# Attention decode with a gated mix: V products and output projection spread over column groups of TensorE, one V buffer instead of a rotation, products taken in their own iteration

## Chip, cores, metric

One core of a Trainium2 chip. The metric is the device time of one execution in microseconds (us). Each run of a kernel has also a span, from its first to its last instruction; in this case the time is the span plus 2.1 to 2.3 us in nearly every run that lists both (669.93 and 667.8, 673.06 and 670.9, 656.03 and 653.9; the largest difference is 2.6), a point that matters below. A profile also lists the clock granted to TensorE as a share of full speed; "half clock" is a stretch in which it is 0.50. Work is called exposed when no transfer runs beside it. All runs quoted are of the fast state, but for one execution of the kernel before of 1794 us, which is left out.

## The reference

```python
q = (x @ wq).reshape(1, 1, 32, 128)                 # x: 1 x 512
scores = einsum('bhqd,bhkd->bhqk', q, k_cache) * 128 ** -0.5   # k_cache: 32 heads x 16384 x 128
a = (softmax(scores) @ v_cache).reshape(1, 1, 4096) @ wo       # v_cache as k_cache
z = gelu(x @ w_in)                                  # 512 x 1792
b = (z1 * (layernorm(z2) * w_sp + b_sp)) @ w_out    # z1, z2: the halves of z
g = sigmoid((x * gate_w).sum())
out = g * a + (1 - g) * b                           # 1 x 512
```

All inputs are bfloat16. The caches are 268 of the 279.7 MB that have to be read.

## The kernel before

The 32 heads are taken in 16 pairs. A pair's K array (128 partitions x 64 KB, 8.39 MB) is multiplied by q on VectorE (DVE) in place, in four pieces; TensorE (PE) sums over d with an identity matrix; DVE reduces the rest; ScalarE (ACT) takes the exponential into `p_t`. Then 64 matmuls with 8 columns each take the product with the pair's V array. Three buffers of 64 KB per partition rotate through K and V, the product of pair i is taken after the scores of pair i + 1, and the products of three pairs are collected together:

```python
def attend(e, v, slot, t0, t1):                     # the V product of one pair
    for t in range(t0, t1):
        ins = e.matmul(d_ps[32 * slot:32 * slot + 8, :], lhsT=p_t[slot][:, 8 * t:8 * t + 8],
                       rhs=v[:, t * 512:(t + 1) * 512], start=(t == 0), stop=(t == NG - 1))
    ...
def pe_pairs(e):
    scores(e, k_buf(0))
    with e.Fori(0, NIT):
        for s in range(SLOTS):
            scores(e, k_buf(s + 1))
            e.wait_ge(exp_s, 1).then_inc(exp_s, -1)
            e.wait_ge(ld_v[s], 16).then_inc(ld_v[s], -16)
            attend(e, v_buf(s), s, 0, NG)
        collect(e)
...
for j, (a, b) in enumerate(zip(WO_CUTS[:-1], WO_CUTS[1:])):     # the end: o @ wo, wo in 4 pieces
    for k in range(a, b):
        for s in range(2):
            y_ok = pe.op(lambda e, k=k, s=s: e.matmul(
                a_ps[s][0:1, 0:256], lhsT=o2[:, k:k + 1],
                rhs=wo[:, k * D + s * 256:k * D + (s + 1) * 256], start=False, ...
```

I call 32 of a matmul's possible output partitions (those from `32 * slot` on, or from 0) a column group; the prediction says, with its source, that they are also columns of the array.

The softmax here doesn't subtract the row's maximum and nothing guards it: scores larger than these inputs give would overflow.

Of the kernel before, what the change touches and what calls it, by code (L numbers as in the profile page):

```python
# [29 lines left out]
SLOTS = 3  # L30
NIT = (NP - 1) // SLOTS
V_CUT = 192
# [36 lines left out]

def gated_mix_kernel(nc, A_x, A_k_cache, A_v_cache, A_wq, A_wo, B_x, B_w_in, B_w_sp, B_b_sp,  # L70
# [7 lines left out]
    buf = [sb(f"buf{b}", [P, ROW], BF16) for b in range(3)]  # L78
    qb = sb("qb", [P, NP * Dh], BF16)
    p_t = [sb(f"p_t{i}", [P, NG * 8], BF16) for i in range(SLOTS)]  # L80
    s_sb = [sb(f"s_sb{i}", [P, KP], FP32) for i in range(2)]
    d_sb = sb("d_sb", [P, 512], FP32)
    x_row = sb("x_row", [1, D], BF16)
    xb = sb("xb", [P, DC * P], BF16)
# [5 lines left out]
    pick = sb("pick", [P, 4 * 2 * SLOTS], FP32)  # L90
    xg = sb("xg", [8, 2 * 64], BF16)
    wb_row = sb("wb_row", [1, 2], BF16)
    xgp = sb("xgp", [8, 64], BF16)
    xgs = sb("xgs", [8, 1], FP32)
# [7 lines left out]
    mv = sb("mv", [P, 2], FP32)  # L102
    var = sb("var", [P, 1], FP32)
    rstd = sb("rstd", [P, 1], FP32)
    z2n = sb("z2n", [P, FhC], FP32)
    u = sb("u", [P, FhC], BF16)
    L_sb = sb("L_sb", [P, H], FP32)
# [5 lines left out]
    res = sb("res", [1, D], BF16)  # L113
# [4 lines left out]
    a_ps = [ps(f"a_ps{i}") for i in range(2)]  # L118
    m_ps = [ps(f"m_ps{i}") for i in range(2)]

    wq = buf[0][:, 0:DC * HDh]
    W_IN = DC * HDh
    W_OUT = W_IN + DC * F
    w_in = buf[0][:, W_IN:W_OUT]
    w_out = buf[0][:, W_OUT:W_OUT + FhC * D]
    wo = buf[0]
# [4 lines left out]
    def k_buf(i):  # L131
        return buf[(2 * i) % 3 if i else 1]

    def v_buf(i):
        return buf[(2 * i) % 3 if i < NP - 1 else 2]

    sem = nc.alloc_semaphore
    ld_x, ld_q, ld_w, ld_s, st_out = (sem(n) for n in ("ld_x", "ld_q", "ld_w", "ld_s", "st_out"))
    ld_k = [sem(f"ld_k{b}") for b in range(3)]
    ld_v = [sem(f"ld_v{b}") for b in range(SLOTS)]  # L140
    ld_e = [sem(f"ld_e{b}") for b in range(2)]
    ld_o = [sem(f"ld_o{b}") for b in range(len(WO_CUTS) - 1)]
    mul_s, red_s, sum_s, exp_s, pv_s, drn_s, col_s = (
        sem(n) for n in ("mul_s", "red_s", "sum_s", "exp_s", "pv_s", "drn_s", "col_s"))
# [7 lines left out]
    for t in [L_sb, *p_t]:  # L152
        p_zero = pool.op(lambda e, t=t: e.memset(t[:, :], 0.0), mark=True)
# [3 lines left out]
    dve.op(lambda e: e.memset(sel[:, :], 0.0), mark=True)  # L157
    const_ok = dve.op(lambda e: e.memset(d_ps[:, :], 0.0), mark=True)

    act.op(lambda e: e.dma_start(out=x_row[:, :], in_=A_x.rearrange("b s d -> (b s) d")),  # L160
           inc=(ld_x, 16))
    sp.op(lambda e: e.dma_start(out=wq, in_=A_wq.rearrange("(p c) n -> p (c n)", c=DC)),
# [4 lines left out]
          inc=(ld_w, 16))  # L167
    sp.op(lambda e: e.dma_start(out=k_buf(0)[:, :], in_=k_src[0]), inc=(ld_k[1], 16))
    sp.op(lambda e: e.dma_start(out=xg[:, 0:64], in_=A_x.rearrange("b s (p d) -> (b s p) d", p=8)),
          inc=(ld_s, 16))  # L170
    sp.op(lambda e: e.dma_start(out=xg[:, 64:128], in_=gate_w.rearrange("(p d) -> p d", p=8)),
          inc=(ld_s, 16))
    sp.op(lambda e: e.dma_start(out=wb_row[:, 0:1], in_=B_w_sp), inc=(ld_s, 16))
    sp.op(lambda e: e.dma_start(out=wb_row[:, 1:2], in_=B_b_sp.rearrange("(a d) -> a d", a=1)),
          inc=(ld_s, 16))
    sp.op(lambda e: e.dma_start(out=k_buf(1)[:, :], in_=k_src[1]), inc=(ld_k[2], 16))
# [7 lines left out]
    for i in range(4):  # L184
# [3 lines left out]
    sel_ok = dve.op(lambda e: e.tensor_copy(  # L188
        out=pick[:, :].rearrange("p (r s q) -> p s q r", r=4, s=SLOTS),
        in_=ident[:, 0:32 * SLOTS].rearrange("p (s x) -> p s x", x=32)[:, :, 0:8]  # L190
        .rearrange("p s (q r) -> p s q r", r=4)), mark=True)

    q_free = [xb_ok, None]
    for n in range(4):
        q_ps = m_ps[n % 2]
        for s in range(2):
            for c in range(DC):
                wait = []
                if s == 0 and c == 0:
                    wait = [w for w in (q_free[n % 2],) if w]  # L200
                    if n == 0:
                        wait += [(ld_q, 16)]
                rhs = (wq[:, c * HDh + n * 1024:c * HDh + (n + 1) * 1024]
                       .rearrange("p (j two d) -> p j two d", two=2, d=Dh)[:, :, s, :])
                q_ok = pe.op(lambda e, q_ps=q_ps, s=s, c=c, rhs=rhs: e.matmul(  # L205
                    q_ps[64 * s:64 * s + 64, :], lhsT=xb[:, c * P:c * P + 64], rhs=rhs,
                    start=(c == 0), stop=(c == DC - 1)), wait=wait, mark=True)
        if n % 2 == 0:
            q_free[0] = dve.op(lambda e, n=n, q_ps=q_ps: e.tensor_copy(  # L209
                out=qb[:, n * 512:(n + 1) * 512], in_=q_ps[:, :]), wait=[q_ok], mark=True)  # L210
        else:
            q_free[1] = act.op(lambda e, n=n, q_ps=q_ps: e.copy(
                out=qb[:, n * 512:(n + 1) * 512], in_=q_ps[:, :]), wait=[q_ok], mark=True)
    qb_ok = list(q_free)

    w_in5 = w_in.rearrange("p (c e m k) -> p c e m k", c=DC, e=2, k=FhC)
    for f in range(FC):
        for c in range(DC):
            z_ok = pe.op(lambda e, f=f, c=c: e.matmul(
                m_ps[0][:, f:f + 1], lhsT=w_in5[:, c, f // FhC, :, f % FhC],  # L220
                rhs=xb[:, c * P:c * P + 1], start=(c == 0), stop=(c == DC - 1)),
                wait=[(ld_w, 32), q_free[0]] if f == 0 and c == 0 else (), mark=True)
    dve.op(lambda e: e.tensor_tensor(out=xgp[:, :], in0=xg[:, 0:64], in1=xg[:, 64:128],  # L223
                                     op=ALU.mult), wait=[(ld_s, 64)], mark=True)
    xgs_ok = dve.chain(lambda e: e.tensor_reduce(out=xgs[:, :], in_=xgp[:, :], axis=AX.X,  # L225
                                                 op=ALU.add))
    pe.op(lambda e: e.matmul(m_ps[1][:, 0:1], lhsT=ones_f[0:8, :], rhs=xgs[:, :], start=True,  # L227
                             stop=True), wait=[xgs_ok, q_free[1]], mark=True)
    g_ok = pe.op(lambda e: e.matmul(m_ps[1][:, 1:3], lhsT=ones_row[0:1, :], rhs=wb_row[0:1, :],
                                    start=True, stop=True), mark=True)  # L230
    act.op(lambda e: e.activation(out=g_sb[:, :], in_=m_ps[1][:, 0:1], func=ACT.Sigmoid),
           wait=[g_ok], mark=True)
    gm_ok = act.op(lambda e: e.activation(out=gm_sb[:, :], in_=m_ps[1][:, 0:1], func=ACT.Sigmoid,
                                          scale=-1.0), mark=True)
    dve.op(lambda e: e.tensor_copy(out=wbf[:, :], in_=m_ps[1][:, 1:3]), wait=[gm_ok], mark=True)
    dve.op(lambda e: e.tensor_copy(out=z[:, :], in_=m_ps[0][:, 0:FC]), wait=[z_ok], mark=True)
# [36 lines left out]
    for k in range(FhC):  # L273
        for s in range(2):
            w_free = pe.op(lambda e, k=k, s=s: e.matmul(  # L275
                a_ps[s][0:1, 0:256], lhsT=u[:, k:k + 1],
                rhs=w_out[:, k * D + s * 256:k * D + (s + 1) * 256], start=(k == 0), stop=False,
                skip_group_check=True), wait=[u_ok] if k == 0 and s == 0 else (), mark=True)

    def scores(e, k):  # L280
        k3 = k[:, :].rearrange("p (j d) -> p j d", d=Dh)
        for c in range(NQ):
            e.wait_ge(mul_s, 1).then_inc(mul_s, -1)  # L283
            for i in range(NS):
                ins = e.matmul(  # L285
                    s_ps[c % 2][:, :].rearrange("p (j w) -> p j w", w=W), lhsT=ident[:, :],
                    rhs=k3[:, c * QK:(c + 1) * QK, i * W:(i + 1) * W],
                    start=(i == 0), stop=(i == NS - 1))
            ins.then_inc(sum_s, 1)

    def attend(e, v, slot, t0, t1):
        for t in range(t0, t1):
            ins = e.matmul(d_ps[32 * slot:32 * slot + 8, :],  # L293
                           lhsT=p_t[slot][:, 8 * t:8 * t + 8],
                           rhs=v[:, t * 512:(t + 1) * 512], start=(t == 0), stop=(t == NG - 1))
        if t1 == NG:
            ins.then_inc(pv_s, 1)

    def collect(e):
        e.wait_ge(drn_s, 1).then_inc(drn_s, -1)  # L300
        for r in range(4):
            ins = e.matmul(o_ps[:, 0:2 * SLOTS], lhsT=d_sb[:, r * Dh:(r + 1) * Dh],  # L302
                           rhs=pick[:, r * 2 * SLOTS:(r + 1) * 2 * SLOTS], start=(r == 0),
                           stop=(r == 3))
        ins.then_inc(col_s, 1)

    def pe_pairs(e):
        e.wait_ge(*sel_ok)
        scores(e, k_buf(0))
        with e.Fori(0, NIT):  # L310
            for s in range(SLOTS):
                scores(e, k_buf(s + 1))
                e.wait_ge(exp_s, 1).then_inc(exp_s, -1)
                e.wait_ge(ld_v[s], 16).then_inc(ld_v[s], -16)
                attend(e, v_buf(s), s, 0, NG)
            collect(e)
# [159 lines left out]
```

## Time and profile before

| | kernel before |
|---|---|
| time, median of 15 runs, the outlier among them | 672.71 us (669.69 to 674.40 without it) |
| the five runs known ahead of the prediction | 673.05 us (671.55 to 674.40) |
| profiled execution | time 669.89 us, span 667.7 us |
| DMA queue busy | 97.0% of 16 engines' span |
| PE / DVE / ACT busy | 76% / 49% / 4% |

### The profile page before, as it was taken

Reading aid. Unit: us, or ns where it says so; the run is one execution under the profiler, and the core shown is the slowest. Engines: PE = TensorE matmul, PEld = TensorE weight load, DVE = VectorE, ACT = ScalarE, POOL = GpSimd, SP = SyncE. Lnnn points to the kernel's source line nnn. Section 1 sums busy time; section 2 is a strip of 40 time slices with the busy share of each in tenths; the row PEclk is TensorE's granted clock in tenths of the full one; section 3 lists DMA queues with packets and bytes.
Section 4 is the critical chain, followed back from the end, with each engine's and each line's share of the span. In section 5 each row is a group of like instructions: output and inputs, shape, how many; then the busy total and the mean of one; then the engine's idle time right before and its main releaser. Section 6 shows DMA issues by size and latency. Waiting matters only on the chain. (4 is left out here: it accounts for less than half of the span.)

```text
span 667.7 us, 5054 instructions
## 1 busy us (share of the span) xinstructions
PE 506.7 (76%) x2278; PEld 211.5 (32%) x2278; DVE 328.9 (49%) x167; ACT 28.0 (4%) x86; POOL 2.2 (0%) x10
## 2 busy tenths in 40 slices
PE   2327598978788796878779597877959787895997
PEld 1213233323233332323334232323423232332344
DVE  1048848274461917456190835629083562809200
ACT  0110000000000000000000000000000000000000
POOL 1000000000000000000000000000000000000000
PEclk9659799989899898989989898998989799898999
DMA  8999999999999999999999999999999999999980
GB/s 367 474 412 421 440 441 432 437 436 437 440 432 428 416 440 436 428 440 436 440 436 432 432 420 436 436 432 436 436 440 436 432 436 416 436 436 436 413 349 0
DMA packets 5807, 279.68 MB, mean 419 GB/s; under 512 B 678, under 2 KB 808, under 8 KB 1064
## 3 DMA queue, kind: packets, MB, share of 16 engines
q1 hardware_dynamic: 5798, 279.58, 97.0%
q8 instruction: 5, 0.08, 0.0%
q14 instruction: 2, 0.02, 0.0%
q10 hardware_dynamic: 2, 0.00, 0.0%
HBM read 279.58 MB, written 0.00 MB: 419 GB/s over the span
## 5 line engine op out<-in xcount | busy, mean ns | idle before, releaser
L327 DVE TENSOR_TENSOR buf<-buf,qb 128x8192 bf16<-128x8192 bf16 x64 | 281.4, 4417 | 187.3 <-DMA buf<-in_A_k_cache_dram 187.3
L285 PE MATMUL s_ps<-buf,ident 128*128 128x512 bf16 x1024 | 255.9, 410 | 118.6 <-PEq L283 118.6
L293 PE MATMUL d_ps<-buf,p_t 128*8 128x512 bf16 x1024 | 223.6, 379 | 0.0
L285 PEld LDWEIGHTS s_ps<-buf,ident 128*128 128x128 bf16 x1024 | 103.1, 104 | 269.9 <-issue 176.1
L293 PEld LDWEIGHTS d_ps<-buf,p_t 128*8 128x8 bf16 x1024 | 87.7, 87 | 134.2 <-issue 6.4
L331 DVE TENSOR_REDUCE s_sb<-s_ps 128x64 f32<-128x512 f32 x64 | 43.9, 686 | 73.2 <-PE s_ps L285 73.2
L339 ACT ACTIVATE p_t<-s_sb 64x256 bf16<-64x256 f32 x32 | 13.3, 415 | 508.7 <-DVE s_sb L331 508.5
L205 PE MATMUL m_ps<-buf,xb 128*64 128x512 bf16 x32 | 6.2, 572 | 10.0 <-DMA buf<-in_A_wq_dram 10.0
L227 PE MATMUL m_ps<-xgs,ones_f 8*128 8x1 f32 x2 | 0.6, 358 | 16.9 <-DVE xgs L225 16.9
L223 DVE TENSOR_TENSOR xgp<-xg 8x64 bf16<-8x64 bf16 x1 | 0.2, 179 | 19.8 <-DMA wb_row<-in_B_b_sp_dram 19.8
L302 PE MATMUL o_ps<-pick,d_sb 128*128 128x6 f32 x48 | 6.2, 253 | 4.6 <-PEq L300 4.6
L302 PEld LDWEIGHTS o_ps<-pick,d_sb 128*128 128x128 f32 x48 | 5.8, 191 | 7.5 <-issue 7.5
L390 DVE RECIPROCAL rl<-m_ps 128x32 f32<-128x32 f32 x1 | 0.4, 359 | 15.3 <-PE m_ps L388 15.3
L209 DVE CAST qb<-m_ps 128x512 bf16<-128x512 f32 x2 | 1.4, 692 | 12.8 <-PE m_ps L205 12.8
L422 PE MATMUL a_ps<-buf,o 128*1 128x256 bf16 x64 | 7.1, 272 | 0.4 <-DVE o L417 0.4
L407 DVE TENSOR_TENSOR o_sb<-o_ps,rl 128x2 bf16<-128x2 f32 x1 | 0.2, 159 | 14.8 <-PE o_ps L302 14.8
L205 PEld LDWEIGHTS m_ps<-buf,xb 128*64 128x64 bf16 x32 | 3.0, 157 | 13.0 <-issue 12.7
L422 PEld LDWEIGHTS a_ps<-buf,o 128*1 128x1 bf16 x64 | 5.3, 84 | 2.0 <-issue 0.5
L339 ACT ACTIVATION_READ_ACCUMULATOR p_t<-s_sb 64x1 f32 x32 | 5.9, 185 | 0.0
L227 PEld LDWEIGHTS m_ps<-xgs,ones_f 8*128 8x128 f32 x2 | 0.5, 308 | 17.0 <-DVE xgs L225 17.0
L369 ACT COPY d_sb<-d_ps 128x512 f32<-128x512 f32 x5 | 2.9, 586 | 60.8 <-PE d_ps L293 60.8
L275 PE MATMUL a_ps<-buf,u 128*1 128x256 bf16 x14 | 3.1, 418 | 2.4 <-DVE u L270 2.4
(66 smaller groups left out, 30.5 us busy)
## 6 DMA issues: line engine op xcount, KB each, us to landing
buf<-in_A_v_cache_dram SPq DMA_DIRECT2D x1, 6144.0 KB, 34.7
buf<-in_A_wq_dram SPq DMA_DIRECT2D x1, 4096.0 KB, 12.3
buf<-in_A_v_cache_dram SPq DMA_DIRECT2D x1, 2048.0 KB, 39.2
buf<-in_A_wo_dram SPq DMA_DIRECT2D x1, 2048.0 KB, 20.3
buf<-in_B_w_in_dram SPq DMA_DIRECT2D x1, 1792.0 KB, 16.2
buf<-in_A_wo_dram SPq DMA_DIRECT2D x1, 1280.0 KB, 23.0
buf<-in_B_w_out_dram SPq DMA_DIRECT2D x1, 896.0 KB, 17.9
buf<-in_A_wo_dram SPq DMA_DIRECT2D x1, 640.0 KB, 24.1
```

Source lines behind the costliest of these rows:

```text
L205: q_ok = pe.op(lambda e, q_ps=q_ps, s=s, c=c, rhs=rhs: e.matmul(q_ps[64 * s:64 * s + 64, :], lhsT=xb[:, c * P:c * P + 64], rhs=rhs, start= ...
L209: q_free[0] = dve.op(lambda e, n=n, q_ps=q_ps: e.tensor_copy(out=qb[:, n * 512:(n + 1) * 512], in_=q_ps[:, :]), wait=[q_ok], mark=True)
L227: pe.op(lambda e: e.matmul(m_ps[1][:, 0:1], lhsT=ones_f[0:8, :], rhs=xgs[:, :], start=True, stop=True), wait=[xgs_ok, q_free[1]], mark=True)
L275: w_free = pe.op(lambda e, k=k, s=s: e.matmul(a_ps[s][0:1, 0:256], lhsT=u[:, k:k + 1], rhs=w_out[:, k * D + s * 256:k * D + (s + 1) * 256] ...
L285: ins = e.matmul(s_ps[c % 2][:, :].rearrange("p (j w) -> p j w", w=W), lhsT=ident[:, :], rhs=k3[:, c * QK:(c + 1) * QK, i * W:(i + 1) * W] ...
L293: ins = e.matmul(d_ps[32 * slot:32 * slot + 8, :], lhsT=p_t[slot][:, 8 * t:8 * t + 8], rhs=v[:, t * 512:(t + 1) * 512], start=(t == 0), st ...
L302: ins = e.matmul(o_ps[:, 0:2 * SLOTS], lhsT=d_sb[:, r * Dh:(r + 1) * Dh], rhs=pick[:, r * 2 * SLOTS:(r + 1) * 2 * SLOTS], start=(r == 0), ...
L327: dve.op(lambda e: e.tensor_tensor(out=k3, in0=k3, in1=q3, op=ALU.mult), wait=wait, inc=(mul_s, 1))
L331: dve.op(lambda e: e.tensor_reduce(out=s_sb[i % 2][:, c * QK:(c + 1) * QK], in_=s_ps[c % 2][:, :].rearrange("p (j w) -> p j w", w=W), axis ...
L339: act.op(lambda e, s=s, rows=rows: e.activation(out=p_t[i % SLOTS][rows, :].rearrange("p (t c) -> p t c", c=8)[:, :, 4 * s:4 * s + 4], in_ ...
L369: act.op(lambda e: e.copy(out=d_sb[:, :], in_=d_ps[:, :]), wait=[(pv_s, i)], inc=(drn_s, 1))
L422: y_ok = pe.op(lambda e, k=k, s=s: e.matmul(a_ps[s][0:1, 0:256], lhsT=o2[:, k:k + 1], rhs=wo[:, k * D + s * 256:k * D + (s + 1) * 256], st ...
```

## The change

The intent: spend less of the end of the kernel on PE after the loads are over. Parts: each V product goes in turn over four column groups; the products are taken in their own iteration and collected pair by pair; K has two buffers and V one; K and V of the last pair come in pieces; the matmuls on `wo` and `w_out` alternate between two column groups; the score matmuls load the identity once per 16; q is projected with full-width matmuls into eight banks; gate loads come first. The core of the diff:

```diff
-    buf = [sb(f"buf{b}", [P, ROW], BF16) for b in range(3)]
+    k_buf = [sb(f"k_buf{b}", [P, ROW], BF16) for b in range(2)]
+    v_buf = sb("v_buf", [P, ROW], BF16)
...
-                ins = e.matmul(
-                    s_ps[c % 2][:, :].rearrange("p (j w) -> p j w", w=W), lhsT=ident[:, :],
-                    rhs=k3[...], start=(i == 0), stop=(i == NS - 1))
+                if i:
+                    ins = matmul_again(nc, e, *args, start=False, stop=(i == NS - 1))  # no weight load
+                else:
+                    ins = e.matmul(args[0], lhsT=args[1], rhs=args[2], start=True, stop=False)
...
+        e.wait_ge(exp_s, 1).then_inc(exp_s, -1)
+        e.matmul(l_ps[:, 0:2], lhsT=ones_f[:, :], rhs=L_sb[:, :], start=True,
+                 stop=True).then_inc(sl_s, 1)
+        for j, (a, b) in enumerate(zip(V_CUTS[:-1], V_CUTS[1:])):
+            e.wait_ge(ld_vp[j], 16).then_inc(ld_vp[j], -16)
+            for t in range(a // 4, b // 4):
+                g = t % 4
+                ins = e.matmul(d_ps[32 * g:32 * g + 8, :], lhsT=p_t[:, 8 * t:8 * t + 8],
+                               rhs=v_buf[:, t * 512:(t + 1) * 512], start=(t < 4),
+                               stop=(t >= NG - 4))
...
+        with e.Fori(0, NP // 2):
+            for b in range(2):
+                scores(e, k_buf[b])
+                attend(e)
...
+            sp.op(lambda e, i=i: e.dma_start(out=v_buf[:, :], in_=v_src[i]),
+                  wait=[(pv_s, i)] if i else [z_ok], inc=(ld_v, 16))   # V(i) waits for product i - 1
...
-                    a_ps[s][0:1, 0:256], lhsT=o2[:, k:k + 1],
+                    a_ps[32 * s:32 * s + 1, 0:256], lhsT=o2[:, k:k + 1],
```

Cut: the q projection, the gate, the pieces of the last pair, the two output transfers.

## The prediction

> **What bounds the kernel now.** I read the page first, parts 2 and 3, for what is busy all the time.
>
> ```profile
> DMA  8999999999999999999999999999999999999980
> GB/s 367 474 412 421 440 441 432 437 436 437 440 432 428 416 440 436 428 440 436 440 436 432 432 420 436 436 432 436 436 440 436 432 436 416 436 436 436 413 349 0
> q1 hardware_dynamic: 5798, 279.58, 97.0%
> ```
>
> The 16 DMA engines are at 90% or more in all slices but the first and the last two. The inputs are 279.7 MB, and no part of the change alters that. The second view is the table of stretches, for the steady rate and for the end:
>
> ```profile
> core 0: us, PE busy (x) PEld busy (x) DVE busy (x) ACT busy (x) POOL busy (x), PEclk, DMA share, GB/s
> 100.00:600.00 500.00, 399.81 (x1722) 161.53 (x1720) 258.28 (x104) 16.17 (x60) 0.00 (x0) 0.93 1.00 434
> 650.10:667.70 17.60, 13.25 (x99) 8.19 (x96) 0.98 (x4) 0.95 (x2) 0.00 (x0) 1.00 0.00 0
> ```
>
> From 100 to 600 us the DMA share is 1.00 at 434 GB/s: for 500 us nothing stalls the transfers, though DVE, PE and the buffers all wait on each other. From 650.1 us on it is 0.00, and 17.6 us of other work follow. So the time is a gapless stream of about 650 us plus a tail, and only the tail, or a new gap in the stream, can change it. The third view is the timeline of the end:
>
> ```profile
> 562.51 0.33 SPq L353 DMA_DIRECT2D buf<-in_A_k_cache_dram  x1
> 562.82 8.76 DVE L327 TENSOR_TENSOR buf<-buf,qb 128x8192 bf16<-128x8192 bf16 x2 [13.52 <-DMA buf<-in_A_k_cache_dram]
> ...
> 588.30 0.18 ACT L339 ACTIVATION_READ_ACCUMULATOR p_t<-s_sb 64x1 f32 x1
> ...
> 624.76 13.98 PE L293 MATMUL d_ps<-buf,p_t 128*8 128x512 bf16 x64
> 624.86 1.75 SPq L386 DMA_DIRECT2D buf<-in_A_wo_dram  x4
> ...
> 640.71 13.98 PE L293 MATMUL d_ps<-buf,p_t 128*8 128x512 bf16 x64
> ...
> 655.45 1.03 PE L302 MATMUL o_ps<-pick,d_sb 128*128 128x6 f32 x8 [0.77 <-PEq L300]
> ...
> 657.93 7.15 PE L422 MATMUL a_ps<-buf,o 128*1 128x256 bf16 x64 [0.40 <-DVE o L417]
> ```
>
> After the last scores (624.8) PE has two V products of 14.0 us in a row (each is 64 matmuls at 14.0/64 = 0.218 us), a collect, and the 64 matmuls on wo, 7.15 us. The last wo piece was issued at about 626.2, and the list of issues gives it 23.9 us to landing, so 650.1. PE's tail alone sets the end from there. The chain of waits agrees: its last 12 us are the collect, some small steps, 7.16 us on a_ps and the cast of the result.
>
> **What the Trainium skill says.** (1) "TensorE: Matmul & The Clock Gate", section "Part 3: Packing small matmuls": outputs at different 32-partition groups use different column groups of the array and run at once; three such tiles of N=512 measured 2.38x. This trace supports it, in the projection of q, whose outputs lie on partitions 0-63 and 64-127:
>
> ```profile
> L205 PE MATMUL m_ps<-buf,xb x32: 379/631/636, 13.2 to 19.0; 128*64 128x512 bf16 x32
> 14.00:15.00 1.00, 1.00 (x8) 0.54 (x6) 0.00 (x0) 0.00 (x0) 0.00 (x0) 1.00 0.90 387
> L293 PE MATMUL d_ps<-buf,p_t x1024: 379/379/379, 91.9 to 654.3; 128*8 128x512 bf16 x171
> ```
>
> The 32 matmuls last 631 ns (slow start) yet start within 5.8 us, 0.19 us apart, and eight touch one microsecond: that is two at a time, for at this slow clock single score matmuls start 0.43 us apart. The V product keeps one pair in one group (partitions 32*slot), so there is no overlap, 0.218 us each. (2) "DMA: Bandwidth & Descriptors", section "Where 436 GB/s comes from": 435 GB/s is the fabric's ceiling; the trace's 434 agrees, so the stream itself can't get faster. (3) The same page, "Anatomy of one DMA": engines don't wait on semaphores, the issuing sequencer does before dispatch; so a late wait on the load queue is a gap only if what it issued earlier has run out. In the trace the queue spends most of the time in waits with the engines at 1.00.
>
> **The change part by part.**
>
> *Fewer buffers for V (one instead of a rotation of three).* V(i+1) is issued only when product i is done, two K buffers alternate. One K or V array is 8.39 MB; at 434 GB/s that is 19.3 us, a pair is 38.7. Let K(i) land at k. Before, from the first multiply to the end of the exponentials it is 588.5 - 562.8 = 25.7 us, and four multiplies of 4.4, four reduces of 0.69 and the score matmuls are all kept. V(i) lands at k + 19.3, earlier, so the product starts at k + 25.7 + 0.4 (the new row-sum matmul on l_ps; the same kind took 0.39). With product time A, V(i+1) is issued at k + 26.1 + A. The stream has K(i+1) to move until k + 38.7. A gap appears when A > 12.6, less about 1 us from issue to first bytes: A > 11.6.
>
> *The V product over four column groups.* At one group A = 14.0 and the stream would have gaps. At 2x it is 7.0, at the skill's 2.38x 5.9, at a full 4x 3.5; load plus matmul pairs of tiny size issue every 3.15/56 = 0.056 us (the z matmuls), so 64 x 0.056 = 3.6 is the floor. I take 4.5 us: a slack of 7 us, no gap.
>
> *Score matmuls without reloading the identity.* Each block of 16 takes 3.61 us = 15 x 0.215 + 0.38 with the loads hidden under the matmuls; nothing to gain but 103 us of load busy time.
>
> *Product in the same iteration, not one later.* It takes one of the two products from the tail.
>
> *Head.* q is now 32 full-width matmuls (no pairs): some 9 us instead of 6.2; but the gate's small loads come first, and the z chain need not wait for 39 us. V(0) is issued after z, at about 28 us by my count (q to 23, evictions 1, z 3.1), and K(1) at about 36. K(0) fills the stream to 39. Close, but covered: no gain, no loss.
>
> *Tail.* Transfers end as before at about 650.1; order K15 (two halves), V15 (three pieces), wo (four). V15 ends at 640.3, K15's first half lands at 611.2, its scores are exponentiated at 611.2 + 25.7 = 636.9, the product of the landed pieces runs from 637.4 to about 641.5, the last 8 matmuls to 642. Then copy and collect (1.75 + waits, as before) to 643.9, the small steps of 1.4 us to 645.3. The wo matmuls now alternate between two column groups: 0.112 us each before, so 0.056 each at full overlap, 3.6 us in all, held to the pieces landing at 645.2, 648.3, 649.8 and 650.1. The end of the last two is about 650.7 (653 if they don't overlap). From there to the end of the span it was 667.74 - 665.09 = 2.65 us. Span 653.4; I add 0.3 for a cold clock or a second output transfer: 653.7, that is 14.0 less than 667.7. Off the median of 673.05 this gives 659.0.
>
> **The rivals.**
> (a) *The single V buffer opens gaps.* If the column groups did not overlap, A = 14.0, each gap would be 14.0 - 11.6 = 2.4 us; a gap also delays K(i+2) and thus hides the next one, so some 1.2 on average, 15 times 18 us: about 677, no better than before. For it: the buffers are fewer and the V issue has only some 7 us of slack instead of the 20 that a V load waits in the queue now. Against it: the q matmuls overlap already.
> (b) *The end of PE, not the transfers, still sets the time*, because the wo matmuls don't overlap, or the PE clock is slow there: end at 652.5 to 653, 661. For it: PE has pauses between the last steps; score matmuls after pauses start 0.43 us apart. Against: between 611 and 668 us the table of stretches has a granted clock of 1.00.
> (c) *The head stalls the stream*, if q takes the slow clock throughout (32 x 0.427 = 13.7 us): V(0) at 32 and K(1) at 40, still covered by V(0) until 58. Then nothing changes.
> (d) *The stream shortens.* There is no idle time in it to remove; at most 0.5 us in the head.
>
> **Range and chances.** The floor is the end of the stream plus about 3 us: 653, or 658.3 in time. Rival (b) costs up to 3 us, small gaps in the stream cost more. 2% better is 659.6 to 659.9, in the middle of this: the mechanism is rather certain, the side of the line is not. I say 659.0, 656.8 to 664.0 in 8 of 10; faster by over 2% 0.56, within 2% 0.41, slower 0.03.
>
> **What would show it.** Right: DMA share 1.00 until about 650 us and a rest of 3 to 4 us; the V product's 64 matmuls in 3.5 to 7 us; each V issue on the queue some 7 us ahead of the K landing; wo's last matmuls ending within 1 us of the last landing; DVE's multiplies still waiting for K. Wrong: dips of the DMA row once every other iteration and a product of 14 us (rival a); wo matmuls 0.11 us apart and an end 2 us later (b); a dip between 28 and 45 us (c). If the stream ends well before 650, my belief that it was already gapless is wrong.

## The result and the profile after

656.03 us, median of 8 runs (655.69 to 656.84), against 672.71 before; ratio 0.9759, 95% interval 0.9743 to 0.9775. A ratio is the mean time of one kernel's fast runs over that of the other's of the same rounds, so not quite the ratio of the medians quoted. Executions over 1.5% slower than the fastest of the same kernel are left out of the means. Faster by over 2%, as held likelier; but 656.03 lies below the range that I gave (656.8 to 664.0).

The page and the table of stretches of the kernel after, for the stream:

```profile
DMA  8999999999999999999999999999999999999996
q1 hardware_dynamic: 6050, 279.58, 98.9%
```

```profile
100.00:600.00 500.00, 284.19 (x1791) 42.50 (x1013) 258.48 (x116) 22.85 (x78) 0.00 (x0) 0.81 1.00 433
650.80:654.90 4.10, 1.33 (x20) 0.74 (x16) 0.41 (x1) 0.36 (x1) 0.00 (x0) 0.92 0.00 0
645.80:652.20 6.40, 6.28 (x64) 3.79 (x64) 0.00 (x0) 0.00 (x0) 0.00 (x0) 0.57 0.45 178
```

The columns are those of the prediction's table: busy time of PE, weight loads, DVE, ACT, POOL, then granted clock, DMA share, GB/s. The stream is as gapless as before and ends at 650.8; the tail behind it is 4.1 us instead of 17.6. In the third line the clock is 0.57: the matmuls on `wo` ran mostly at half clock here. The timeline of the loop and of the end:

```profile
569.69 3.63 PE L306 MATMUL d_ps<-v_buf,p_t 128*8 128x512 bf16 x64
573.36 0.33 SPq L364 DMA_DIRECT2D v_buf<-in_A_v_cache_dram  x1
582.16 4.43 DVE L335 TENSOR_TENSOR k_buf<-k_buf,qb 128x8192 bf16<-128x8192 bf16 x1 [13.96 <-DMA k_buf<-in_A_k_cache_dram]
...
637.95 3.69 PE L306 MATMUL d_ps<-v_buf,p_t 128*8 128x512 bf16 x64
...
645.85 6.28 PE L417 MATMUL a_ps<-k_buf,o 128*1 128x256 bf16 x64 [1.36 <-DMA k_buf<-in_A_wo_dram]
```

A V product takes 3.63 us here instead of 13.98. The next V is issued when it is done, at 573.4; the K in flight lands at 582.16 (the DVE line: it starts when K is there), so the queue is 8.8 us ahead. The chain of waits now names a transfer, that of the first piece of wo, and behind it the matmuls at mostly half clock:

```profile
612.82 32.99 DMA k_buf<-in_A_wo_dram
645.81 0.04 issue
645.85 6.33 PE a_ps L417 x64
```

So the mechanism is as predicted. What is 3 us off is the time. The predicted span was 653.7; the spans of the ten runs of the kernel after are 653.6 to 654.9.

### The profile page after: what moved, and what is told of

It is laid out like the page before. It is cut to its first block, busy times and chain, and to the rows that moved or that the text cites.

```text
span 654.9 us, 4444 instructions
## 1 busy us (share of the span) xinstructions
PE 373.8 (57%) x2388; PEld 61.8 (9%) x1400; DVE 332.8 (51%) x188; ACT 37.1 (6%) x112; POOL 1.2 (0%) x8
## 5 line engine op out<-in xcount | busy, mean ns | idle before, releaser
L335 DVE TENSOR_TENSOR k_buf<-k_buf,qb 128x8192 bf16<-128x8192 bf16 x64 | 282.4, 4414 | 207.2 <-DMA k_buf<-in_A_k_cache_dram 207.2
L74 PE MATMUL s_ps<-k_buf,ident 128*128 128x512 bf16 x960 | 249.2, 418 | 0.0
L295 PE MATMUL s_ps<-k_buf,ident 128*128 128x512 bf16 x64 | 27.5, 429 | 214.0 <-PEq L288 214.0
L306 PE MATMUL d_ps<-v_buf,p_t 128*8 128x512 bf16 x1024 | 68.1, 426 | 0.0
L295 PEld LDWEIGHTS s_ps<-k_buf,ident 128*128 128x128 bf16 x64 | 6.3, 98 | 415.8 <-issue 415.8
L306 PEld LDWEIGHTS d_ps<-v_buf,p_t 128*8 128x8 bf16 x1024 | 25.7, 94 | 34.5 <-issue 13.8
L312 PE MATMUL o_ps<-pick,d_sb 128*128 128x2 f32 x128 | 16.4, 250 | 12.5 <-PEq L310 12.5
L300 PE MATMUL l_ps<-L_sb,ones_f 128*128 128x2 f32 x32 | 5.7, 249 | 30.9 <-PEq L299 30.9
L312 PEld LDWEIGHTS o_ps<-pick,d_sb 128*128 128x128 f32 x128 | 15.5, 191 | 20.1 <-issue 20.1
L387 ACT COPY d_sb<-d_ps 128x512 f32<-128x512 f32 x15 | 8.8, 585 | 71.7 <-PE d_ps L306 71.7
L417 PE MATMUL a_ps<-k_buf,o 128*1 128x256 bf16 x64 | 6.3, 388 | 1.4 <-DMA k_buf<-in_A_wo_dram 1.4
```

The lines of the kernel that those rows point to most:

```text
L74: ins = eng.matmul(out, lhsT=lhsT, rhs=rhs, **flags).ins
L295: ins = e.matmul(args[0], lhsT=args[1], rhs=args[2], start=True, stop=False)
L300: e.matmul(l_ps[:, 0:2], lhsT=ones_f[:, :], rhs=L_sb[:, :], start=True, stop=True).then_inc(sl_s, 1)
L306: ins = e.matmul(d_ps[32 * g:32 * g + 8, :], lhsT=p_t[:, 8 * t:8 * t + 8], rhs=v_buf[:, t * 512:(t + 1) * 512], start=(t < 4), stop=(t >= ...
L312: ins = e.matmul(o_ps[:, 0:2], lhsT=d_sb[:, r * Dh:(r + 1) * Dh], rhs=pick[:, r * 2:(r + 1) * 2], start=(r == 0), stop=(r == 3))
L335: dve.op(lambda e: e.tensor_tensor(out=k3, in0=k3, in1=q3, op=ALU.mult), wait=wait, inc=(mul_s, 1))
```

## The experiments

**The kernel before again.** No edit; 14 runs.

> The kernel before, unchanged, to see why its median of 672.7 us lies 3 us above its profiled execution (669.9 us, span 667.7), which is the 3 us that my prediction missed: span predicted 653.7, found 653.6 to 654.7, but I subtracted a difference of spans from the median. Theory A (clock phase): the end of this kernel hangs on PE and DVE from the last K landing (601.5) on, and stretches of half clock on PE fall in it differently from run to run; spans 667.5 to 672, and a profile that is slower than the first one has the same last landing of wo (650 within 0.5) and the same DMA share 1.00, but a later start of the last two V products, with a slow score block behind the last K landing. Theory B (transfers): the stream itself ends 2 to 3 us later in the typical run; then wo's last landing moves with the span. The new kernel's runs spread by only 1.2 us with the same stream, which speaks for A.

672.72 us (669.93 to 674.79), spans 667.8 to 672.6; only one of the 14 is as short as the profile that I predicted from. This run's own profile (span 670.9) shows the difference:

```profile
625.06 13.98 PE L293 MATMUL d_ps<-buf,p_t 128*8 128x512 bf16 x64
625.16 1.75 SPq L386 DMA_DIRECT2D buf<-in_A_wo_dram  x4
...
641.00 13.98 PE L293 MATMUL d_ps<-buf,p_t 128*8 128x512 bf16 x64
...
658.24 10.00 PE L422 MATMUL a_ps<-buf,o 128*1 128x256 bf16 x64 [0.40 <-DVE o L417]
```

```profile
657.90:664.10 6.20, 5.86 (x28) 3.52 (x29) 0.19 (x1) 0.00 (x0) 0.00 (x0) 0.50 0.00 0
664.10:668.30 4.20, 4.13 (x38) 2.94 (x35) 0.03 (x1) 0.03 (x1) 0.00 (x0) 1.00 0.00 0
```

The last piece of wo lands at the same 650.1 as before (issued at 626.5, 23.6 us to landing), so theory B falls for this run. But theory A was right only in kind: the two products start just 0.3 us later, and the rest comes where I did not look, in the matmuls on wo: 10.00 us, 6.2 of them with a granted clock of 0.50, against 7.15 at 1.00. 0.3 + 2.85 is the 3.2 us between the two spans.

**Useless matmuls to hold the clock, in every iteration of the kernel before.**

```diff
                 attend(e, v_buf(s), s, 0, NG)
+                warm(e, 21)      # 21 matmuls of the identity with q into an idle bank
```

> The kernel before with 21 matmuls of no use after each V product (4.5 us at full clock, in the pause of PE before the next scores), so that PE's clock does not fall. Theory A: the first score block of a pair no longer runs at half clock, spread falls to about 1 us and the median to 668.5 to 670.5, 2 to 4 us less than before of the same rounds. Theory B: no change of median and spread (672 to 673).

675.36 us (674.02 to 676.92), ratio 1.0043: a faulty experiment. The last 21 sit between the second last product and its collect, where nothing was idle: the last product starts at 646.2 instead of 640.7. It can't tell the two theories apart. It does show that filled pauses go with a higher clock: 0.96 on average over its runs, against 0.92 before. A better test of the theories stands further below, in the tail of this kernel.

**One column group.** The kernel after, but:

```diff
-                g = t % 4
+                g = 0            # start and stop flags to match
```

> The new kernel with all 64 matmuls of a V product in one column group (the one V buffer kept). My theory: product 14.0 instead of 3.6 us, V is issued about 40 us after its K has landed, 1 to 2 us after the next K has landed, so the DMA row has gaps; stream end later by 10 to 25 us, and the last product is exposed too: 672 to 684 us, no better than the kernel before. Rival (the column groups don't matter, the new order of loads and products does it): product as before 14 us but time 656 to 662.

700.32 us, ratio 1.0427: slower than the kernel before, and by more than expected. Timeline and page:

```profile
598.42 13.98 PE L306 MATMUL d_ps<-v_buf,p_t 128*8 128x512 bf16 x64
612.42 0.33 SPq L364 DMA_DIRECT2D v_buf<-in_A_v_cache_dram  x1
...
613.40 4.42 DVE L335 TENSOR_TENSOR k_buf<-k_buf,qb 128x8192 bf16<-128x8192 bf16 x1 [16.47 <-DMA k_buf<-in_A_k_cache_dram]
```

```profile
DMA  8999798999999899998999979899899999989992
```

V is issued at 612.42, 1.0 us ahead of the landing of K at 613.40, and yet lands 21.4 us after that K (634.8) where a full queue takes 19.35. Over this run's loads: issued 3.8 us ahead of the landing before it, 19.34; 1.0 us ahead, 20.7; 1.2 us behind, 23.0. So a load must be issued some 3 us ahead; I had allowed 1 us (start of the first transfer after its issue). The last piece of wo lands, and so the stream ends, at 685.3, 34.5 us later than in the kernel after, and the exposed last product adds the rest. The rival falls: without the column groups, one V buffer makes this kernel worse than the one before.

**Column groups alone.** The kernel before with each product in turn over the four groups, collected by itself; nothing else of the change:

```diff
+            g = t % 4        # flags, copies and the pick matrix to match
-            ins = e.matmul(d_ps[32 * slot:32 * slot + 8, :], ...
+            ins = e.matmul(d_ps[32 * g:32 * g + 8, :], ...
...
                 attend(e, v_buf(s), s, 0, NG)
-            collect(e)
+                collect(e)
```

> The kernel before with one part of the change alone: each V product over four column groups and collected by itself; three rotating buffers, product one pair late, wo matmuls in one group, weights reloaded, all as before. My theory: the two products of the tail shrink from 28 to 7.3 us and their first runs beside transfers, so the end is the stream (650.1) plus wo's 64 matmuls one by one from 645.2 (7.2 us, up to 13 at half clock): span 654 to 660, time 656.5 to 662; nearly all of the gain. Rival (the gain needs the new buffers and the piecewise loads): 664 or more.

659.74 us (659.10 to 660.05), ratio 0.9815 (0.9792 to 0.9837, so on which side of 2% it lies is unclear): 12.7 of the 16.7 us.

```profile
624.88 3.63 PE L294 MATMUL d_ps<-buf,p_t 128*8 128x512 bf16 x64
...
644.95 9.79 PE L422 MATMUL a_ps<-buf,o 128*1 128x256 bf16 x64 [0.84 <-DMA buf<-in_A_wo_dram]
```

The product is as short as in the kernel after; the matmuls on wo, one by one, end at 654.7, 4.9 us after the last landing.

**Runs of 16 to a group.** The kernel after with the same four groups in another order:

```diff
-                g = t % 4
+                g = t // 16      # start and stop flags to match
```

> The new kernel with the same four column groups, but the 64 matmuls of a V product in four runs of 16 to one group instead of in turn. If matmuls start in program order and overlap only with a neighbour in another group, just the seams overlap: product near 13.3 us and the time as with one group (700.3), 695 to 701. If PE reaches ahead past matmuls of the same group (the paired starts in the q projection of the kernel before, whose program has four in a row to one group, hint at some reach), product 3.6 to 8 us and 656 to 660.

688.79 us (687.31 to 689.94), ratio 1.0247: between the one-group kernel and the kernel after, and in neither of the two ranges that I gave. Products take 11.40 us, or 13.01 where the clock is low at first:

```profile
548.15 11.40 PE L306 MATMUL d_ps<-v_buf,p_t 128*8 128x512 bf16 x64
...
588.14 13.01 PE L306 MATMUL d_ps<-v_buf,p_t 128*8 128x512 bf16 x64
```

Two lines count the matmuls that touch 0.1 us of the last product (after the stretch and its length: PE busy with the count, clock, DMA share, GB/s). They show two inside a run (each lasts 0.379 and starts 0.216 after the one before) and four at a seam:

```profile
667.30:667.40 0.10, 0.10 (x4) 1.00 0.24 102
668.15:668.25 0.10, 0.10 (x2) 1.00 0.48 205
```

By the start times in the trace, four matmuls at each of the three seams have a partner that starts with them: 64 - 3 x 4 = 52 starts x 0.216 = 11.2 us, near the 11.40 found. As two of one group never start together (the one-group kernel has 13.98 for 64), the partners must be of the next group, started while up to four of the old one were still to come. The trace does not say which matmul of the program a record is, so this is a conclusion from the counts. A run of four should then overlap fully; the last run tests that.

**Matmuls on wo in one group.** The kernel after, but both halves on partition 0, in two halves of one bank, the two result copies one after the other (0.4 us):

```diff
-                    a_ps[32 * s:32 * s + 1, 0:256], lhsT=o2[:, k:k + 1],
+                    a_ps[0:1, s * 256:(s + 1) * 256], lhsT=o2[:, k:k + 1],
```

> The new kernel with the matmuls on wo (and on w_out) all in column group 0, in two halves of one bank; the two copies of the result are put one after the other for that (0.4 us more). My theory: the 64 matmuls on wo take 7.2 us at full clock, some 10 at the mixed clock seen in the kernel with the V groups alone (9.8), instead of 6.3, so they end at 653 to 656 instead of 652.2: 657.5 to 660.5. Rival (they hide behind the pieces of wo anyway): 656.0 to 656.6.

659.90 us (659.58 to 660.69), ratio 0.9826. Its result is wrong (relative error 0.26): both halves open an accumulation in the same bank and partitions. The Trainium skill, "PSUM — Partial Sum Buffer", section "Terms", says that the opening matmul clears the written bits of the whole bank for these partitions, so the second opening drops the first half's first term. One lost term of seven in half of the outputs would be an error of about sqrt(1/14) = 0.27, if the error is a ratio of norms; no run here isolates it. No instruction depends on the values, so the time stands.

```profile
647.17 7.15 PE L417 MATMUL a_ps<-k_buf,o 128*1 128x256 bf16 x64 [0.40 <-DVE o L412]
```

It is 3.9 us over the kernel after, 0.4 of them the copies: the second column group is worth some 3.5 us at the end. The rival falls.

**Useless matmuls in the pauses at the end of the kernel after.** The first three stand in `attend`, so they run after every V product and not only the last.

```diff
         ins.then_inc(pv_s, 1)
+        warm(e, 3)
...
+    pe.raw(lambda e: warm(e, 2))     # ahead of the transpose of o
...
+    pe.raw(lambda e: warm(e, 6))     # ahead of the matmuls on wo
```

> The new kernel with a few matmuls of no use in the pauses of PE between the V product and the matmuls on wo, so that the latter run at full clock (in the profile of the new kernel they ran at half clock, 0.213 us a pair, for most of 6.3 us). If half clock costs there, the last matmul ends within 0.5 us of wo's last landing: 654.8 to 655.5, 0.6 to 1.1 less than the new kernel's 656.0. Rival: no change, as the pieces of wo pace them.

655.96 us (655.77 to 656.47), ratio 0.9765 to before: no gain over 656.03. In its profile the matmuls do what I said, at a clock of 1.00, and end at 650.7, 0.5 us after the landing of the last piece (650.2):

```profile
645.37 1.91 PE L424 MATMUL a_ps<-k_buf,o 128*1 128x256 bf16 x32
648.38 1.25 PE L424 MATMUL a_ps<-k_buf,o 128*1 128x256 bf16 x20 [1.10 <-DMA k_buf<-in_A_wo_dram]
649.92 0.82 PE L424 MATMUL a_ps<-k_buf,o 128*1 128x256 bf16 x12 [0.28 <-DMA k_buf<-in_A_wo_dram]
```

But its spans are 653.5 to 654.4, and those of the kernel after 653.6 to 654.9, of which the profile was the longest. That profile was a bad guide: to judge by the spans, half clock in these matmuls costs the kernel after about 1 us in its slowest runs only. The profile of the last run below, at a usual 655.95 us, agrees: there 52 of them take 3.00 us and the last 12 take 0.82.

**The same in the tail of the kernel before**, seven matmuls.

```diff
         attend(e, v_buf(NP - 1), 0, V_CUT // 4, NG)
+        warm(e, 3)
         collect(e)
...                               # and 1, 1, 2 ahead of the transpose, of o2 and of wo
```

> The kernel before with seven matmuls of no use in PE's pauses after the last V product (at most one us of delay if they are in the way). In its second profile (span 670.9) the stream ended as in the first (650.1) but the matmuls on wo took 10.0 us instead of 7.15 as they fell partly on half clock; that is the missing 3 us. If this is the cause: median 669.5 to 670.8 instead of 672.5 and a spread below 2 us instead of 4.4. If the spread comes from elsewhere: 672 to 674 and the same spread.

670.37 us (669.68 to 671.70) in 22 runs, against 672.52 (669.67 to 674.66) of the same rounds; ratio 0.9976 (0.9967 to 0.9985). Spread 2.0 us instead of 5.0, and the median comes down by 2.15.

```profile
641.64 13.98 PE L293 MATMUL d_ps<-buf,p_t 128*8 128x512 bf16 x64
...
658.93 7.15 PE L430 MATMUL a_ps<-buf,o 128*1 128x256 bf16 x64
```

So most of the 3 us between the first profile and the usual run is half clock in the matmuls on wo. What spread remains goes with the start of the last product (641.64 here, 640.71 in the first profile). Of these 0.9 us, 0.6 are transfers, as theory B had it: the last K lands at 602.1 instead of 601.5. The other 0.3 are a longer first block of scores (8.75 instead of 8.44). I did not test that further.

**Groups for V and for wo, the rest as before.** The kernel of "column groups alone" plus:

```diff
-                    a_ps[s][0:1, 0:256], lhsT=o2[:, k:k + 1],
+                    a_ps[s][32 * s:32 * s + 1, 0:256], lhsT=o2[:, k:k + 1],   # and for w_out
```

> The kernel before with two parts of the change: the V products over four column groups (as in the run of that part alone, 659.7 us) and the matmuls on wo over two. Buffers, order of the products, q, gate loads, reloaded weights stay as before. If these two parts are the whole gain: 655.3 to 656.5 us, the new kernel's 656.0 within 0.1%. If the rest of the change (one V buffer, product at once, pieces of K15 and V15, head, no reloads) is worth something: 657.5 or more.

656.30 us (655.47 to 658.18), ratio 0.9764: the kernel after within its spread. All other parts of the change together are not seen in the time.

```profile
645.20 6.54 PE L422 MATMUL a_ps<-buf,o 128*1 128x256 bf16 x64 [0.64 <-DMA buf<-in_A_wo_dram]
```

**The same with the useless matmuls in the tail.**

> The same with the few matmuls of no use in PE's pauses at the end. The stream of the kernel before ends at 650.1, 0.7 us before that of the new kernel (650.8), so with the wo matmuls at full clock the end is 650.1 + 0.5 + 2.7: 653.3, time 655.0 to 655.6, a little under both kernels. If half clock no longer costs here: as the run without them.

655.68 us (655.32 to 656.55), ratio 0.9754 (0.9736 to 0.9772). The lowest median of all, but its interval covers the kernel after's 0.9759: no better version is shown, only an equal one with three rotating buffers.

**Two groups for V.** The kernel after with `g = t % 2`.

> The new kernel with each V product in turn over two column groups instead of four. Product 7.0 us (32 x 0.216), V issued 33 us after its K has landed, 5 us before the next has: no gap in the stream, unlike with one group (700.3). Only the last product is exposed, 3.4 us longer, less 1.1 us of slack ahead of wo: 657 to 660.

661.77 us (659.10 to 664.02), ratio 0.9852, above what I expected: of four runs just the profiled one, the fastest, lies in the range. Products take 7.1 us at full clock, 8.6 to 8.8 where it is low at first, and then V's lead over the landing ahead of it can shrink to less than 3 us:

```profile
76.24 0.33 SPq L364 DMA_DIRECT2D v_buf<-in_A_v_cache_dram  x1
...
79.08 4.42 DVE L335 TENSOR_TENSOR k_buf<-k_buf,qb 128x8192 bf16<-128x8192 bf16 x1 [13.12 <-DMA k_buf<-in_A_k_cache_dram]
```

In this profile the last piece of wo lands at 653.6 instead of 650.8, in spite of no full gap: issues 2.8 us ahead cost once 0.8 and once 1.9 us, issues 3.3 us or more ahead at most 0.3. The other three runs are 2.0 to 4.9 us slower and have no profile.

**Runs of four to a group.** The kernel after with `g = (t // 4) % 4`.

> The new kernel with the V matmuls in runs of four to a column group, the groups in turn. With runs of 16 the trace shows four pairs at each seam, so PE seems to start up to four later matmuls of another group ahead of time. If so, runs of four pair up throughout: product 6.9 us (or less, if it reaches two groups ahead), time 656 to 660. If order is strict, only every fourth overlaps: 64 x 0.216 x 3/4 = 10.4 us, time 660 to 672.

655.89 us (655.73 to 656.64), ratio 0.9756, as the kernel after.

```profile
608.44 3.66 PE L306 MATMUL d_ps<-v_buf,p_t 128*8 128x512 bf16 x64
```

Full overlap of four groups, though four matmuls in a row name the same one: PE starts later matmuls of another group ahead of earlier ones (strict order would take 10.4 us by the estimate above). A look-ahead of a fixed four matmuls would not give this, as the four that start together lie up to 12 apart in the program; up to four matmuls waiting at each group would fit this run and the one with runs of 16, but no run tests that rule. The same would explain the pairs in the q projection of the kernel before, whose program has four in a row to each half.

## Why the prediction was right or wrong

1. *The stream is gapless and sets the floor, about 650 us*: right, 650.8. DMA share 1.00 from 100 to 600 us before and after.
2. *The V product shrinks to 4.5 us*: right in kind, better in size: 3.63 at full clock, up to 5.31 where the clock is low at first. The evidence used, the pairs in the q projection, was good; why they pair was found only here. One of its lines needs care: it gives the clock as 1.00 where the pairs start 0.427 us apart. In the kernel after the single matmuls of that projection start 0.427 apart too and then, within the same 9 us, 0.216, so the clock was low and the column wrong there. The 3.63 fits both four at a time (16 x 0.216, and 0.16 for the end of the last) and the prediction's floor of 3.6 for issuing loads and matmuls; the runs don't separate the two.
3. *A slack of 7 us at each V issue*: right, 6.3 to 9.9 us from the second V on. The head was right too: V(0) is issued at 27.6 us and K(1) at 34.0, without a dip.
4. *Without column groups about 677 (rival a)*: rightly seen as the danger, wrong in size: 700.3. A load needs some 3 us of lead instead of the 1 us that I took, and I left out the last product, exposed at the end.
5. *The tail ends at 650.7, span 653.4, 0.3 added, 653.7*: right, the runs have spans of 653.6 to 654.9. There is some luck in the last tenths: the stream ended at 650.2 to 650.8 in the four profiles with the new buffering that keep four column groups in turn or in fours, not at 650.1, and the 0.3 that was added for other reasons makes up for most of that. The profiled one has its last matmul at 652.2, by half clock, as rival (b) said in part.
6. *"Off the median of 673.05 this gives 659.0"*: this step failed, and with it the range: its floor 658.3 came the same way (653 + 5.3), and the lower end, 656.8, was not set far enough below it. I subtracted the difference of two spans, 667.7 - 653.7, from a median, as if the profile showed the median run. It showed one of the fastest: time 669.89, 2.2 us above its span. The right step was 653.7 + 2.2 = 655.9, found 656.03; the gain against the usual run is 16.7 us, not 14.0. The term that was too small is the tail of the kernel before: 17.6 us behind the stream in the profile used, 20.8 in the second one (650.1 to 670.9). What lies behind the missing 3 us was not in the profile at hand: the matmuls on wo, exposed behind the stream, can run partly at half clock (10.0 us against 7.15 in the second profile). That this is so in most runs of the kernel before is shown by holding the clock up there, which takes 2.15 us off the median. The change hides these matmuls behind the landings of wo, so it removes most of that cost and of its spread.
7. *The other parts are worth nothing*: right: V groups 12.7 us, wo groups 3.4 more (659.74 to 656.30, on different chips), the rest not seen.

## What to carry to other kernels

Where one engine's stream is gapless, count what runs after it ends, and shorten or overlap just that; here two edits that spread narrow matmuls over column groups gave all of the gain, and the new buffering none. Predict the changed kernel's time from its own floor and tail plus the fixed difference of time and span, not by subtracting from a median what was worked out on a profile, unless the profiled run is a median one. If a kernel's runs spread and a stretch of PE work stands exposed at its end, ask in which clock it ran in that profile.

## What the Trainium skill lacked or had wrong

- "TensorE: Matmul & The Clock Gate", section "Part 3: Packing small matmuls — row/col tiling", has no measured figure for four column tiles alone, and says that matmuls start in strict program order. Here four groups with 8 columns and N = 512 took 3.63 us for 64 matmuls against 13.98 in one group, 3.85 times; and runs of four to one group overlapped as well (3.66), runs of 16 by four at each seam (11.40), which strict order does not give.
- "DMA: Bandwidth & Descriptors", section "Where 436 GB/s comes from", says without a condition that for loads from HBM the HBM side binds at about 358 GB/s. Here a program on one core read 434 GB/s for 500 us. The same page, under its measured sizes, keeps the 358 for two cores that stream at once; the sentence lacks that condition. The page also has no figure for how far ahead a load must be issued to keep a queue of 8.39 MB loads full: some 3 us here (3.3 us ahead or more: at most 0.3 us lost; 1.0 ahead: 1.4 to 2.0).
- "TensorE: Matmul & The Clock Gate", Part 1, has no figure for what half clock costs from run to run at the end of a kernel: here spans of 667.8 to 672.6 us for the same program, and in two profiles 7.15 and 10.00 us for the same 64 exposed matmuls.
